# Moving the first group's values to GpSimd's queue in an attention-and-experts kernel: cast in the transfer, sink rows by a second transfer, mask fills on VectorE

## The chip, the cores and the metric

The kernel runs on one core of a Trainium2 chip. The engines are TensorE (PE), VectorE (DVE), ScalarE (ACT), GpSimd (POOL) and SyncE (SP, which only requests transfers here); 16 DMA engines move data for all of them. The metric is the device time in microseconds of one execution, smaller is better; the median of three runs is given, and a profile of one further execution.

## The reference, cut to what matters

Two parts follow each other. The first is attention over 4 batches, 8 heads, 768 positions and head width 64; the second is a mixture of 4 experts over the 3072 resulting rows.

```python
mask   = where(is_retrieval, causal, causal & (is_sink | in_window))   # 4 sinks, window 64
a      = softmax(where(mask, q @ k.T / sqrt(64), -1e9))
x      = (a @ v)                      # -> (3072, 512) rows, heads side by side
p      = probs / (probs.sum(-1) + 1e-9)
out    = sum_e p[:, e] * (relu(x @ w1[e]) @ w2[e])     # w1[e] 512x1024, w2[e] 1024x512
```

Heads 0, 2 and 6 are retrieval heads (all earlier positions); heads 1, 3, 4, 5 and 7 are streaming heads (a window of 64, and the first 4 positions, the sinks).

## The kernel before

All inputs are float32 in DRAM, and the matmuls run in float16. The attention is cut into eight groups: a batch and half of its 768 rows (384 rows) each. The first group, batch 0 and rows 0 to 383, is the front of the program: nothing can hide it, since the experts need its output. From then on the experts' matmuls are the main stream of PE, and the steps of the other groups are put between them by a planner (`plan`, `due`) at fixed places of the program. Each engine works through its own instructions strictly in the order of the program, and waits by semaphores.

**The front.** `front()` runs a list of steps written out by hand (`FRONT`): casts of q and k from float32 rows (x), transposes of them by PE (t), copies of these into place (c), scores and exponentials (s), products with the values (v and p), and what follows them (r, l, t, y, m). Names such as ck1 mean a step and its head or pair. For pairs of streaming heads the step p first multiplies by the halves of the value tiles that hold ones, to get the sums, and then by the values: p1 for heads 1 and 5, p3 for 3 and 7; v4, v0, v6 and v2 are the others. PE takes them in the order p1, v4, v0, v6, v2, p3. The masks are added to the scores as biases `bC` (causal) and `bS` (window), which live in the tile `early`; PE adds them by a matmul with the identity `ident16`.

**Tiles of the values.** `vR` holds the retrieval heads' values, and `vS` the streaming heads'. A tile of vS has 128 rows: rows 32 to 127 are 96 positions (R0 is 32), rows 0 to 3 repeat the sinks, which are the first four positions of the head, and the rest of rows 0 to 31 must only hold finite numbers. One half of the columns is the head's 64 values, the other half holds a constant for the sums. 

**Values of the first group before.** SyncE requests them as float32 into a staging area in `hA` (`request_v`, L437 and L439), after q's (asked by ScalarE) and k's float32 rows (L454). The sinks of all heads come into `v_s32` in one small transfer (L470), and GpSimd copies them to the staging rows of every tile (`put_sinks_of_v`, L430). VectorE fills the rows 0 to 31 of the staging area with zeros first (L490). GpSimd then casts head after head into vS and vR (`cast_v`, L450), with the requests of w1(0), the first layer's weights of expert 0, between the casts.

**GpSimd's queue.** Everything that is cast on the way (weights, later q, k and v) is requested by GpSimd, in one fixed order: w1(0) in two halves of two transfers (L330), w2(0) (L354), fills for group 1 (L381), w1(1), q and k of group 1 (L232), w2(1), w1(2), values of group 1 (`load_v`, L306 and L312), and so on. `landed` makes GpSimd wait until a tile has arrived. Requests of one kind of queue use eight completion semaphores in turn, so the ninth waits until the first has landed; that holds for GpSimd's requests and, together, for those of SyncE and ScalarE. Before the values GpSimd builds the masks: it fills them and cuts them with selects (L506 to L558).

**VectorE at the start** fills the warm-up tile (L416), the ones in vR and vS, the keys' tile kS (L381), the staging zeros (L490) and `x_one`; then it takes the steps of the front.

Of the kernel before, what the change touches and what calls it, by code (L numbers as in the profile page):

```python
# [11 lines left out]
FP32 = mybir.dt.float32  # L12
FP16 = mybir.dt.float16
AF = mybir.ActivationFunctionType
ALU = mybir.AluOpType
# [4 lines left out]
def kernel(  # L20
# [33 lines left out]
    nc = tc.nc  # L54
    P = 128
    B, H, S, D = q.shape
# [4 lines left out]
    HP = H // 2  # L61
# [6 lines left out]
    RETR = (1, 0, 1, 0, 0, 0, 1, 0)  # L68

    PLACE = [(h % HP, h // HP) for h in range(H)]  # L70
    RH = [h for h in range(H) if RETR[h]]
    SH = [h for h in range(H) if not RETR[h]]
    NS = int(n_sink)
    NW = int(window)
    TK = 96
    R0 = P - TK
    TQ = TK + NW
    NT = S // TK
    TC = CH // TK
# [18 lines left out]
    gp = nc.gpsimd  # L98
# [8 lines left out]
    NR, NSH = len(RH), len(SH)  # L107
# [9 lines left out]
    hA = pers.tile([P, 5 * KT * P], FP16, name="hA")  # L117
# [12 lines left out]
    vS = vSf.rearrange("p (c t s x) -> p c t s x", c=NCH, t=TC, s=NSH)  # L130

    def windows(x):

        return x[:, 0 : WT * NSH * P].rearrange("p (t s x) -> p t s x", t=WT, s=NSH)

    ident16 = pers.tile([P, P], FP16, name="ident16")

    XS = 3 * DMP * 2 * P
    early = moe.tile([P, XS], FP16, name="early", tag="xs", bufs=1)
    warm = early[:, 1024:1536]  # L140
    bC = early[:, 1536:1792]
    bS = early[:, 1792:2272].rearrange("p (t x) -> p t x", t=3)
# [27 lines left out]
    def half(u):  # L170
        return slice(u * D, (u + 1) * D)
# [5 lines left out]
    def own_v(h):  # L177
        return half(PLACE[h][1])
# [10 lines left out]
    def v_tiles(b, c, h):  # L189

        if RETR[h]:
            return vR[b % 2][:, 3 * c : 3 * c + 3, RH.index(h), :]
        if b:
            return windows(vSf)[:, :, SH.index(h), :]
        return vS[:, c, :, SH.index(h), :]
# [10 lines left out]
    def rows_of(x, b, h, c):  # L206
        return x[b, h, c * CH : (c + 1) * CH, :].rearrange("(j p) d -> p j d", p=P)

    def tiles_of(x, b, h, c):
        return x[b, h, c * CH : (c + 1) * CH, :].rearrange("(t r) d -> r t d", r=TK)  # L210

    def windows_of(x, b, h, c):

        assert b > 0
        first = ((b * H + h) * S + c * CH - WO) * D
        return bass.AP(x.tensor, x.offset + first, [[D, P], [WQ * D, WT], [1, D]])
# [85 lines left out]
    def load_v(b, c, heads):  # L302
        for h in heads:
            t = v_tiles(b, c, h)
            if RETR[h]:
                gp.dma_start(out=t[:, :, 0:D], in_=rows_of(v, b, h, c))  # L306
            elif b:
                gp.dma_start(  # L308
                    out=t[:, :, own_v(h)], in_=windows_of(v, b, h, c)
                )  # L310
            else:
                gp.dma_start(  # L312
                    out=t[R0:P, :, own_v(h)],
                    in_=tiles_of(v, b, h, c),
                )

    def sink_rows(b, c):
# [3 lines left out]
        for t in range(TC):  # L321
            nc.sync.dma_start(
                out=vS[0:NS, c, t, :, :], in_=vS[R0 : R0 + NS, 0, 0, :, :]
            )

    def load_w1(e, chunks=(0, 2)):
        x = moe_w1[e].rearrange("(u c d) f -> u d c f", u=2, c=DMP)
        for c in chunks:
            for u in range(2):
                gp.dma_start(  # L330
                    out=w1sb[half(u), e * DMP + c : e * DMP + c + 2, :],
                    in_=x[u, :, c : c + 2, :],
                )
# [33 lines left out]
    ONES = 0.0078125 * (1.0 + 15360.0 * 2.0**-23)  # L367
# [3 lines left out]
    def fill(eng, ap, value):  # L371
        ap = ap.bitcast(FP32)
        if eng is nc.scalar:
            src = ones[0 : ap.shape[0], :]
            if len(ap.shape) == 3:
                src = src.rearrange("p (a b) -> p a b", a=1)
            elif len(ap.shape) == 4:
                src = src.rearrange("p (a b c) -> p a b c", a=1, b=1)
            eng.copy(out=ap, in_=src.to_broadcast(list(ap.shape)))
        else:  # L380
            eng.memset(ap, value)  # L381
# [11 lines left out]
    def one_values_r(eng, i, c):  # L393
        t = slice(3 * c, 3 * c + 3)
        fill(eng, vR[i][:, t, :, D : D + 2], ONES)

    def one_values(eng, c):

        one_values_r(eng, 0, c)
        x = vS[:, c, :, :, :]  # L400
        if c:
            fill(eng, x[0:R0, :, :, :].rearrange("p t s x -> p (t s x)"), ONES)
        fill(eng, x[:, :, 0:2, D:P], ONES)
        fill(eng, x[:, :, 2:5, 0:D], ONES)

# [6 lines left out]
        return x.rearrange("p (s x) -> p s x", s=HP)  # L412

    q32, k32 = rows32(0), rows32(1)
    for x in (warm[:, 0:P], warm[:, P:]):
        nc.vector.memset(x.bitcast(FP32), 0.0)  # L416
    v32 = hA[:, 12 * H * D :].bitcast(FP32)
    vR32 = v32[:, 0 : NR * 3 * D].rearrange("p (n j d) -> p n j d", n=NR, j=3)
    vS32 = v32[:, NR * 3 * D : (NR * 3 + NSH * TC) * D]
    zeros = vS32[0:R0, :]  # L420
    vS32 = vS32.rearrange("p (n t d) -> p n t d", n=NSH, t=TC)

    STAGE = (1, 3, 5, 7, 4)

    v_s32 = early[0:NS, 0:1024].bitcast(FP32).rearrange("p (h d) -> p h d", h=H)

    def put_sinks_of_v():
        for n, m, x in ((0, HP, v_s32[:, 1:H:2, :]), (HP, 1, v_s32[:, HP : HP + 1, :])):
            x = x.rearrange("p n (t d) -> p n t d", t=1)
            gp.tensor_copy(  # L430
                out=vS32[0:NS, n : n + m, :, :], in_=x.to_broadcast([NS, m, TC, D])
            )

    def request_v(eng, heads):
        for h in heads:
            if RETR[h]:
                eng.dma_start(out=vR32[:, RH.index(h), :, :], in_=rows_of(v, 0, h, 0))  # L437
            else:
                eng.dma_start(  # L439
                    out=vS32[R0:P, STAGE.index(h), :, :], in_=tiles_of(v, 0, h, 0)  # L440
                )

    def cast_v(eng, heads):
        for h in heads:
            if RETR[h]:
                out_, in_ = v_tiles(0, 0, h)[:, :, 0:D], vR32[:, RH.index(h), :, :]
            else:
                out_ = v_tiles(0, 0, h)[:, :, own_v(h)]
                in_ = vS32[:, STAGE.index(h), :, :]
            eng.tensor_copy(out=out_, in_=in_)  # L450

    def request_triples(eng, x, x32, s):
        y = x[0, 2 * s : 2 * s + 2, 0:CH, :]
        eng.dma_start(  # L454
# [4 lines left out]
    for s in (0, 2, 1, 3):  # L459
# [7 lines left out]
    )  # L467
    request_triples(nc.sync, k, k32, 0)
    request_triples(nc.sync, k, k32, 2)
    nc.sync.dma_start(out=v_s32, in_=v[0, :, 0:NS, :].rearrange("h r d -> r h d"))  # L470
    request_triples(nc.sync, k, k32, 1)
    request_triples(nc.sync, k, k32, 3)
    request_v(nc.sync, (1, 5, 4, 0, 6, 2, 3, 7))
    nothing = warm.bitcast(FP32)[:, 0:1]
    x = kR[0][:, 0, :, :, :].rearrange("p n t x -> p (n t x)").bitcast(FP32)
    nc.scalar.copy(out=x, in_=nothing.to_broadcast(list(x.shape)))
    nc.sync.dma_start(
        out=probs,
        in_=moe_domain_probs[0 : NPL * P, :].rearrange("(t p) e -> p t e", p=P),
    )  # L480
    nc.sync.dma_start(
        out=p_in.rearrange("t x e -> t (x e)"),
        in_=moe_domain_probs.rearrange("(t x) e -> t (x e)", x=P),
    )
    nc.vector.memset(eps, 1e-9)
    nc.vector.memset(ones, ONES)
    make_identity(nc, ident16)
    one_values(nc.vector, 0)
    zero_keys(nc.vector, 0)
    nc.vector.memset(zeros, 0.0)  # L490


    ps_warm = pO.tile([P, DM], FP32, name="pO", bufs=2)
# [7 lines left out]

    def mask_c(x, keep, drop):

        gp.memset(x, keep)  # L506
        for i in range(2):
            gp.affine_select(
                out=x[:, i * P : (i + 1) * P], in_=x[:, i * P : (i + 1) * P],
                compare_op=ALU.is_ge, fill=drop, base=0, pattern=[[1, P]],  # L510
                channel_multiplier=-1,
            )

    def mask_s(x, n, keep, drop):

        gp.memset(x, keep)
        gp.affine_select(
            out=x, in_=x, compare_op=ALU.is_ge, fill=drop,
            base=R0, pattern=[[0, n], [1, TQ]], channel_multiplier=-1,
        )  # L520
        gp.affine_select(
            out=x, in_=x, compare_op=ALU.is_ge, fill=drop,
            base=NW - 1 - R0, pattern=[[0, n], [-1, TQ]], channel_multiplier=1,
        )
        gp.memset(x[0:R0, :, :], drop)
        gp.memset(x[0:NS, :, 0:TK], keep)
        gp.affine_select(
            out=x[0:NS, 0, 0:TK], in_=x[0:NS, 0, 0:TK], compare_op=ALU.is_ge,
            fill=drop, base=-NW, pattern=[[1, TK]], channel_multiplier=-1,
        )  # L530

    def mask_w():
# [20 lines left out]
            base=WQ - WF - NW, pattern=[[1, WQ]], channel_multiplier=-1,  # L553
        )

    mask_c(bC, 0.0, -60000.0)
    mask_s(bS[:, 0:2, :], 2, 0.0, -60000.0)
    gp.tensor_copy(out=bS[:, 2, :], in_=bS[:, 1, :])  # L558
    put_sinks_of_v()
    k16 = moe.tile([P, H, 3, D], FP16, name="k16", tag="pB", bufs=1)  # L560
    qt16 = att.tile([P, H, 3, D], FP16, name="q16", bufs=1)

# [9 lines left out]
        return w2sb[0:1, (e + 1) * FTP - 1, 0:1]  # L572


    cast_v(gp, (1,))
    load_w1(0, (0,))
    cast_v(gp, (5, 4, 0))
    load_w1(0, (2,))
    cast_v(gp, (6, 2, 3, 7))
    load_w2(0)  # L580
    zero(gp, kR[0][:, 1, :, :, :])
    zero_keys(gp, 1)
# [1254 lines left out]
```

## Time and profile before

| what | us |
|---|---|
| median of 3 runs | 373.56 (372.93 to 374.04) |
| the profiled execution | 373.37 |
| its span (first to last instruction) | 371.6 |
| PE busy | 365.0 |
| VectorE busy | 279.8 |
| ScalarE busy | 227.0 |
| GpSimd busy | 118.7 |
| granted clock of TensorE | 1.0 throughout |

The page gives busy times for the whole span, and the span in 40 slices of 9.3 us, as tenths. The trace can also be asked for one engine's instructions in order of time (the timeline), for the chain of work that ended last, and for who waited for whom. In the timeline a line gives the start, the length, the engine, the line of the program, the operation, the tiles, and in brackets the idle time just before with what ended it. Matmuls are pipelined, so a busy PE is not PE at its peak.

### The profile page before, as it was taken

What the parts mean: (1) busy time and instruction counts of PE and PEld (TensorE: products, weight loads), DVE (VectorE), ACT (ScalarE), POOL (GpSimd) and SP (SyncE); (2) the same over time, 40 slices, a digit from 0 to 9 for tenths busy, and PEclk for the clock granted to TensorE, in tenths of its full rate; (3) what the DMA queues carried; (4) which work ended last, traced back from release to release, by engine and by line L of the source; (5) the groups of instructions that cost most, each with busy time, mean ns of one, the idle gap of its engine ahead of it and who ended that gap; (6) DMA issues with size and microseconds to landing.
All of it is one profiled execution on the core that took longest, in us unless ns stands there. A gap on an engine that the chain in (4) does not pass through costs nothing.

```text
span 371.6 us, 10363 instructions
## 1 busy us (share of the span) xinstructions
PE 365.0 (98%) x4240; PEld 310.4 (84%) x4240; DVE 279.8 (75%) x586; ACT 227.0 (61%) x476; POOL 118.7 (32%) x173
## 2 busy tenths in 40 slices
PE   8999999999999999999999999999999999999996
PEld 5744566578998989999989899998899998998996
DVE  7864785898697589778657849867768868979882
ACT  6735779357777785775776856774777361451630
POOL 6975656784075049026402740220000000000000
PEclk9999999999999999999999999999999999999999
DMA  8999999999999399969906991960220300300101
GB/s 220 176 194 208 174 198 172 188 195 131 125 110 152 87 104 145 141 98 90 175 11 76 157 152 27 127 127 6 73 69 2 114 3 2 116 2 10 50 3 56
DMA packets 119716, 39.65 MB, mean 107 GB/s; under 512 B 107648, under 2 KB 112324, under 8 KB 119668
## 3 DMA queue, kind: packets, MB, share of 16 engines
q0 software_dynamic: 82816, 18.62, 58.8%
q1 hardware_dynamic: 35764, 19.58, 25.2%
q10 hardware_dynamic: 1088, 0.79, 0.7%
q8 instruction: 33, 0.54, 0.6%
q14 instruction: 15, 0.12, 0.1%
HBM read 44.89 MB, written 6.34 MB: 138 GB/s over the span
## 4 chain that ended last, share of the span: by engine, by line
PE 82%; DMA 11%; POOL 4%; DVE 1%; issue 1%; ACT 0%; SPq 0%; POOLq 0%
PE pO L1569 31%; PE pA L1386 23%; PE pO L1415 9%; DMA w1sb<-in_moe_w_dram 5%; PE pA L893 4%; PE pO L1269 3%; PE pA L1224 3%; DMA q<-in_q_dram 2%; PE pV L1415 2%; PE pA L1415 2%; DMA w2sb<-in_moe_w_dram 2%; POOL w1sb L330 2%; PE pV L1003 2%; PE pV L951 2%; DMA hA<-in_v_dram 1%; DMA hA<-in_q_dram 1%
## 5 line engine op out<-in xcount | busy, mean ns | idle before, releaser
L1569 PEld LDWEIGHTS <-hA 128*128 128x128 f16 x1104 | 104.8, 98 | 11.9
L1386 PE MATMUL pA<-xs,w1sb 128*128 128x256 f16 x768 | 97.1, 272 | 0.0
L1386 PEld LDWEIGHTS <-w1sb 128*128 128x128 f16 x768 | 71.7, 98 | 7.3
L1569 PE MATMUL pO<-w2sb,hA 128*128 128x256 f16 x640 | 76.8, 272 | 0.0
L1395 ACT ACTIVATE hA<-pA 128x512 f16<-128x512 f32 x96 | 57.2, 598 | 28.9 <-PE pA L1386 26.6
L911 ACT ACTIVATE es<-pA 128x384 f16<-128x384 f32 (+2 forms) x122 | 58.3, 513 | 25.0 <-PE pA L893 22.1
L308 POOL DMA_DIRECT2D vS<-in_v_dram x30 | 29.6, 988 | 106.6 <-PE pV L1003 106.0
L1569 PE MATMUL pO<-tsb,hA 128*128 128x256 f16 x464 | 56.8, 272 | 0.0
L1334 DVE TENSOR_TENSOR xs<-xT,pB 128x1024 f16<-128x1024 f16 (+1 forms) x49 | 47.5, 987 | 1.9 <-DMA vS<-in_v_dram 1.9
L1152 DVE TENSOR_TENSOR hA<-hA 128x1024 f16<-128x1024 f16 x60 | 39.4, 685 | 0.6 <-PE pO L1569 0.3
L1251 ACT ACTIVATE hA<-pA 128x128 f16<-128x128 f32 (+1 forms) x61 | 20.4, 381 | 20.4 <-PE pA L1224 20.1
L1415 PEld LDWEIGHTS <-w1sb 128*128 128x128 f16 x512 | 31.4, 98 | 1.4 <-issue 0.5
L1224 PE MATMUL pA<-xT,w1sb 128*128 128x128 f16 (+1 forms) x244 | 29.3, 270 | 0.5 <-DMA w1sb<-in_moe_w_dram 0.5
L1269 PE MATMUL pO<-w2sb,hA 128*128 128x512 f16 x120 | 28.6, 379 | 1.1 <-DMA w2sb<-in_moe_w_dram 1.1
L1589 ACT COPY s<-pO 128x256 f32<-128x256 f32 x31 | 11.6, 373 | 27.3 <-PE pO L1569 21.8
L1224 PEld LDWEIGHTS <-w1sb 128*128 128x128 f16 x256 | 19.3, 98 | 9.7 <-issue 1.8
L1024 DVE TENSOR_TENSOR xT<-pV,rc 64x384 f16<-64x384 f32 x35 | 19.4, 555 | 9.5 <-ACT rc L1021 8.9
L1432 DVE CUSTOM_DVE_ANT_0 hA<-pO,s 128x512 f16<-128x512 f32 x26 | 17.7, 688 | 9.8 <-PE pO L1415 8.5
L922 DVE TENSOR_TENSOR es<-es,mS 128x384 f16<-128x384 f16 (+1 forms) x40 | 13.6, 345 | 14.9 <-ACT es L911 14.8
L1425 ACT COPY s<-pO 128x512 f32<-128x512 f32 x39 | 22.7, 587 | 3.2 <-PE pO L1415 3.0
L1018 ACT ACTIVATE rc<-pV,eps 64x384 f32<-64x384 f32 x35 | 20.2, 576 | 6.3 <-PE pV L1003 5.7
L1269 PEld LDWEIGHTS <-hA 128*128 128x128 f16 x128 | 12.1, 98 | 13.6 <-issue 1.6
(189 smaller groups left out, 545.6 us busy)
## 6 DMA issues: line engine op xcount, KB each, us to landing
pB<-p_rows SPq DMA_DIRECT2D x10, 512.0 KB
out_dram<-o SPq DMA_DIRECT2D x19, 256.0 KB
w1sb<-in_moe_w_dram POOLq DMA_DIRECT2D x16, 256.0 KB, 7.2
w2sb<-in_moe_w_dram POOLq DMA_DIRECT2D x8, 512.0 KB, 9.4
vS<-in_v_dram POOLq DMA_DIRECT2D x30, 112.0 KB, 4.8
k_rows<-in_k_dram POOLq DMA_DIRECT2D x18, 128.0 KB, 5.6
q<-in_q_dram POOLq DMA_DIRECT2D x18, 128.0 KB, 6.5
out_dram<-hA SPq DMA_DIRECT2D x4, 256.0 KB
```

Source lines behind the costliest of these rows:

```text
L308: gp.dma_start(out=t[:, :, own_v(h)], in_=windows_of(v, b, h, c))
L911: nc.scalar.activation(out=es[:, 0:cols], in_=ps[:, 0:cols], func=AF.Exp, scale=SC)
L1152: nc.vector.tensor_tensor(out=out, in0=a, in1=b, op=ALU.subtract)
L1224: nc.tensor.matmul(out=ps[:, 0 : x.shape[2]], lhsT=w1_tile(e, CTS[n], ft), rhs=x[:, CTS[n], :], start=(n == 0), stop=(n == DMP - 1),)
L1251: nc.scalar.activation(out=hs[:, ft, :], in_=ps[:, 0:cols_n], func=AF.Relu)
L1269: nc.tensor.matmul(out=ps_o, lhsT=hs[:, ft, j * P : (j + 1) * P], rhs=w2sb[:, e * FTP + ft, :], start=(ft == 0), stop=(ft == FTP - 1),)
L1334: nc.vector.tensor_tensor(out=o, in0=xin, in1=pb.to_broadcast([P, DMP, n, P]), op=ALU.mult)
L1386: nc.tensor.matmul(out=ps[:, f * PC : (f + 1) * PC], lhsT=w1_tile(e, ct, f0 + f), rhs=xs[:, ct, :], start=(ct == 0), stop=(ct == DMP - 1),)
L1395: nc.scalar.activation(out=blocks[:, b0 : b0 + 2, k0 : k0 + 2, :].rearrange("p t f x -> p f t x"), in_=ps.rearrange("p (f t x) -> p f t x" ...
L1415: nc.tensor.matmul(out=ps[:, f * P : (f + 1) * P], lhsT=w_tile(e, w[:, ct, :], f), rhs=a[:, ct, :], start=(first and f == 0 and ct == 0), ...
L1425: nc.scalar.copy(out=kept[n], in_=ps)
L1569: nc.tensor.matmul(out=ps, lhsT=a[:, k, :], rhs=b(k), start=(first and k == 0), stop=(k == KT - 1), skip_group_check=not first,)
```

## The change

The values of the first group no longer pass a staging area. GpSimd requests them straight from DRAM into vS and vR, and the transfer casts them (`load_v(0, 0, ...)`). Their sinks are copied by SyncE, head by head, out of the landed rows 32 to 35 of the head's first tile into rows 0 to 3 of all four tiles (`own_sinks`), for heads 1, 5, 4, 3 and 7. VectorE fills rows 0 to 31 of vS with the constant that the ones have. The identity's and masks' fills, and two copies inside the masks, go to VectorE; GpSimd keeps the selects, and no longer builds the causal mask twice. The requests stand in this order on GpSimd: select of the identity, three selects of the masks, heads 1 and 5, the select of the first sinks, heads 4 and 0, w1(0)'s first half, heads 3, 7, 6, 2, w1(0)'s second half, w2(0). Everything behind this is in the same order as before on every engine; the lines of the new program are some 26 lower from there on (L1224 becomes L1198).

```diff
+    def own_sinks(h):
+        x = vS[:, 0, :, SH.index(h), own_v(h)]
+        src = x[R0 : R0 + NS, 0:1, :]
+        nc.sync.dma_start(out=x[0:NS, :, :], in_=src.to_broadcast([NS, TC, D]))
...
-        if c:
-            fill(eng, x[0:R0, :, :, :].rearrange("p t s x -> p (t s x)"), ONES)
+        fill(eng, x[0:R0, :, :, :].rearrange("p t s x -> p (t s x)"), ONES)
...
-    for x in (warm[:, 0:P], warm[:, P:]):
+    masks = early[:, 1536:2272]
+    for x in (warm[:, 0:P], warm[:, P:], ident16, masks):
         nc.vector.memset(x.bitcast(FP32), 0.0)
...
-    nc.sync.dma_start(out=v_s32, in_=v[0, :, 0:NS, :].rearrange("h r d -> r h d"))
     request_triples(nc.sync, k, k32, 1)
     request_triples(nc.sync, k, k32, 3)
-    request_v(nc.sync, (1, 5, 4, 0, 6, 2, 3, 7))
...
-    make_identity(nc, ident16)
+    make_identity(nc, ident16, nomemset=True)
     one_values(nc.vector, 0)
     zero_keys(nc.vector, 0)
-    nc.vector.memset(zeros, 0.0)
...
+    def mask_c():
+        x = bC[:, 0:P]
+        gp.affine_select(out=x, in_=x, compare_op=ALU.is_ge, fill=DROP, ...)
+        nc.vector.tensor_copy(out=bC[:, P : 2 * P], in_=x)
+    def mask_s():
+        x = bS[:, 0:2, :]
+        gp.affine_select(...)        # two selects, as before
+        nc.vector.memset(x[0:R0, :, :], DROP)
+        nc.vector.memset(x[0:NS, :, 0:TK], 0.0)
+        nc.vector.tensor_copy(out=bS[:, 2, :], in_=bS[:, 1, :])
+    def mask_first_sinks():
+        x = bS[0:NS, 0, 0:TK]
+        gp.affine_select(...)        # one select, as before
...
-    mask_c(bC, 0.0, -60000.0)
-    mask_s(bS[:, 0:2, :], 2, 0.0, -60000.0)
-    gp.tensor_copy(out=bS[:, 2, :], in_=bS[:, 1, :])
-    put_sinks_of_v()
+    mask_c()
+    mask_s()
+    load_v(0, 0, (1, 5))
+    mask_first_sinks()
+    load_v(0, 0, (4, 0))
...
-    cast_v(gp, (1,))
     load_w1(0, (0,))
-    cast_v(gp, (5, 4, 0))
+    load_v(0, 0, (3, 7, 6, 2))
     load_w1(0, (2,))
-    cast_v(gp, (6, 2, 3, 7))
+    for h in (1, 5, 4, 3, 7):
+        own_sinks(h)
     load_w2(0)
```

More of the change, by code (lines that the diff above doesn't have):

```diff
@@ L414 @@
     q32, k32 = rows32(0), rows32(1)
-    for x in (warm[:, 0:P], warm[:, P:]):
+    masks = early[:, 1536:2272]
+    for x in (warm[:, 0:P], warm[:, P:], ident16, masks):
         nc.vector.memset(x.bitcast(FP32), 0.0)
[L417 to L450, printed above, removed]
     def request_triples(eng, x, x32, s):
@@ L500, in warm_up @@
             )
[L504 to L516, printed above, removed]
-        gp.affine_select(
-            out=x, in_=x, compare_op=ALU.is_ge, fill=drop,
-            base=R0, pattern=[[0, n], [1, TQ]], channel_multiplier=-1,
+    DROP = -60000.0
+    def mask_c():
+        x = bC[:, 0:P]
+        gp.affine_select(
+            out=x, in_=x, compare_op=ALU.is_ge, fill=DROP, base=0,
+            pattern=[[1, P]], channel_multiplier=-1,
+        )
+        nc.vector.tensor_copy(out=bC[:, P : 2 * P], in_=x)
+    def mask_s():
+        x = bS[:, 0:2, :]
+        gp.affine_select(
+            out=x, in_=x, compare_op=ALU.is_ge, fill=DROP,
+            base=R0, pattern=[[0, 2], [1, TQ]], channel_multiplier=-1,
         )
         gp.affine_select(
-            out=x, in_=x, compare_op=ALU.is_ge, fill=drop,
-            base=NW - 1 - R0, pattern=[[0, n], [-1, TQ]], channel_multiplier=1,
-        )
-        gp.memset(x[0:R0, :, :], drop)
-        gp.memset(x[0:NS, :, 0:TK], keep)
+            out=x, in_=x, compare_op=ALU.is_ge, fill=DROP,
+            base=NW - 1 - R0, pattern=[[0, 2], [-1, TQ]], channel_multiplier=1,
+        )
+        nc.vector.memset(x[0:R0, :, :], DROP)
[3 more added lines that the diff above has]
+        x = bS[0:NS, 0, 0:TK]
         gp.affine_select(
-            out=x[0:NS, 0, 0:TK], in_=x[0:NS, 0, 0:TK], compare_op=ALU.is_ge,
-            fill=drop, base=-NW, pattern=[[1, TK]], channel_multiplier=-1,
+            out=x, in_=x, compare_op=ALU.is_ge, fill=DROP, base=-NW,
+            pattern=[[1, TK]], channel_multiplier=-1,
         )
```

## The prediction

> **What bounds the kernel now.** I read the page first: its span and the slices.
>
> ```profile
> span 371.6 us, 10363 instructions
> PE   8999999999999999999999999999999999999996
> DMA  8999999999999399969906991960220300300101
> ```
>
> TensorE (PE) is full from the first slice on, DMA for the first 15 slices of 9.3 us. A change in the first 20 us can only move the end if it moves PE. So I read PE's timeline from 10 to 62 us for every idle stretch that a transfer or an engine ended.
>
> ```profile
> 11.51 0.44 PE L734 MATMUL pO<-es,vS 128*64 128x160 f16 x7 [0.16 <-POOL vS L450]
> ...
> 24.82 1.89 PE L1269 MATMUL pO<-w2sb,hA 128*128 128x512 f16 x8 [0.47 <-DMA w2sb<-in_moe_w_dram]
> ...
> 30.11 2.76 PE L1224 MATMUL pA<-xT,w1sb 128*128 128x384 f16 x16 [0.30 <-DMA w1sb<-in_moe_w_dram]
> ...
> 37.56 1.89 PE L1269 MATMUL pO<-w2sb,hA 128*128 128x512 f16 x8 [0.61 <-DMA w2sb<-in_moe_w_dram]
> ...
> 59.69 0.49 PE L1224 MATMUL pA<-xT,w1sb 128*128 128x384 f16 x2 [0.24 <-DMA w1sb<-in_moe_w_dram]
> ```
>
> In brackets stands the idle time before an instruction and what ended it. PE starts the MoE's first matmul at 17.2 and waits for weights four times: 0.47 + 0.30 + 0.61 + 0.24 = 1.62 us. These waits are the cushion of everything below: a PE that leaves the front later meets weights that are there. After 59.7 the chain of waits is PE nearly without a break. Up to there it runs through transfers (start, length, what):
>
> ```profile
> 4.65 4.38 DMA hA<-in_v_dram
> 9.15 0.47 POOL vS L450
> ...
> 23.00 9.10 DMA q<-in_q_dram
> ...
> 34.43 8.03 DMA w1sb<-in_moe_w_dram
> 42.74 6.41 DMA w2sb<-in_moe_w_dram
> 49.44 10.12 DMA w1sb<-in_moe_w_dram
> ```
>
> So the weights' order is paced by GpSimd's (POOL's) queue, whose first pieces wait for the values. Last, VectorE (DVE) at the start:
>
> ```profile
> 3.47 1.12 DVE L490 MEMSET hA<- 32x1280 f32 x1 [0.20 <-issue]
> 4.57 0.14 DVE L1716 MEMSET x_one<- 128x96 uint32 x1
> 4.63 0.28 DVE L631 CAST t1sb<-hA 128x384 f16<-128x384 f32 x1
> 5.87 0.56 DVE L658 CAST kS<-pA 64x384 f16<-64x384 f32 x1 [0.95 <-PE pA L642]
> ```
>
> The first cast of keys starts when DVE's fills end, with no wait for the landing: the fills set the start of the front (PE begins its transposes at 4.97).
>
> **VectorE.** Removed: the zeros of the staging rows, 1.12. Added in its place: the ones in vS's first 32 rows, the same 32x1280 shape, 1.12. These cancel. Added besides: fills of 64 and 368 columns, 320 columns by 32 rows, 96 columns by 4 rows, and copies of 128 and 160 columns. A 1280-column fill takes 1.12 and a 96-column one 0.14, so about 0.06 + 0.83 ns a column, and the 0.06 is mostly hidden behind the next. Fills: 0.06 + 0.31 + 0.33 + 0.14 = 0.84. The copies: the cast of 384 columns takes 0.28, POOL's own copy of 160 columns 0.31. So 0.1 to 0.3 each; I take 0.15, since DVE does them, 0.3 for both. Two of these wait for the one before on the same engine, 0.05 each. Sum 1.2 (0.9 to 1.6). POOL's selects between them are done by 3.1, ahead of DVE's need at 5. The first cast therefore starts at 5.85, not 4.63. Behind it stand tk0, ck1, the scores and the eight exponentials that keep ScalarE (ACT) full from 7.46 to 10.24. ACT is the limit of that stretch, so DVE's later 0.36 of waiting for keys doesn't give the time back. Front +1.2.
>
> **SyncE.** Removed: nine requests of values. The fourth key request no longer waits for a q landing (the chain shows it sent at 4.24). The keys land earlier, but behind a DVE that reaches them only at 9.7 this gives nothing.
>
> **GpSimd.** Removed: nine fills, selects and copies of masks or sinks, and eight casts (five of 0.42, three of 0.36). Added: eight requests at the row of the same transfer in group 1 (L312, 0.68; L306, 0.75). Its new times: three selects from 1.4 to 3.1 (0.29 + 2 x 0.46 and gaps). The request of head 1 waits for DVE's ones in vS, to 3.75. Heads 1 and 5 go by 5.1. The select of the first sinks waits for DVE's last fill, near 5.65, and everything behind it on POOL with it: heads 4 and 0 at 6.2 to 7.6. Then w1(0)'s first half 7.6 to 8.95 (9.70 before), 3, 7, 6, 2 to 11.8, the second half to 13 (13.2 before). w2(0) must wait until w1(0)'s first piece has landed, because eight completion counters are used in turn: 7.6 + 6.3 (that request's own landing before) = 13.9, then two requests of 0.72 to 15.3 (15.9 before). The fills and w1(1) behind come 0.6 earlier. DMA is full in this time, so what is gained is the stretch before 9.7 in which w1 wasn't yet asked for: weights earlier by 0.6 to 2. That is enough to hold the cushion, and PE can't use more.
>
> **The values' way.** Before, PE waited 0.16 for POOL's cast of head 5 (0.3 with the weight load); this goes. Now heads 1, 5, 4 (then 3, 7) need a landing and then a second transfer for the sinks. A values transfer of this size took 4.7 to 8.8 from request to landing at 40 to 46 us; the shortest of the same line family (L308, 112 KB, at 245 us) took 3.3. At 4 to 8 us the engines still finish q and k, at 324 GB/s to 7 us. I take 4.2, nearer to the quiet row, since little is queued ahead. Head 1 lands at 8, 5 at 8.6, 4 at 10.3. The second hop: SyncE's copies of sinks in group 1 (L322) issue in 0.58; the last store of the kernel goes out at 369.1 and the span ends at 371.6, 2.5; the early sinks (L470, asked for at 1.83, in POOL's hands at 5.83) took 4.0. I take 2.7. Sinks of 1, 5, 4 at 10.7, 11.3, 13.0. PE wants the first two at 11.2 + 1.2 = 12.4 (no wait) and head 4 at 11.55 + 1.2 = 12.75. Expected wait 0.5, as the end is uncertain by 1 both ways and a wait can't be below 0. Heads 3 and 7 travel behind w1's first half in POOL's one queue: landing 15, sinks of 7 at 18; PE wants them near 17.9. Again about 0.5.
>
> *A page beside this.* The Trainium skill, "DMA: Bandwidth & Descriptors", section "Anatomy of one DMA", gives a POOL-issued transfer 2.0 us and its bytes. By it, as an estimate, head 4 would have its sinks at about 11.5, both waits fall out, and the sum below would be -0.6 (373.0, inside the forecast's own range). The rows from 40 to 46 us, 4.7 and more, speak for the longer way.
>
> **Sum.** Front: +1.2 - 0.2 + 0.5 + 0.5 = +2.0. Less the cushion 1.62: +0.4 at 59.7 us, and PE carries it to the end. The profiled execution took 373.37 (1.77 around the span), so 373.8; the median of the runs, 373.56, is 0.19 above it: 374.0.
>
> **Rivals.** *The second hop becomes the wait (slower).* At the upper ends, head 4 lands at 11.9 (5.6, as one such load at 40 us) and the hop takes 3.0: sinks at 14.9, PE 2.2 late there; heads 3 and 7 add 0.5. Front +3.7, end +2.1: 375.7. It decides from a front delay of 2.7 (2.7 - 1.62 = 1.1). For it: PE takes its instructions in order, so nothing passes the waiting matmuls, and DMA is full. Against it: the quiet 3.3.
>
> *The fills are cheap and the weights come earlier (faster).* If DVE overlaps its small fills (0.6 in all) and no value is late, the front costs +0.4 and the cushion's 1.62 is nearly all gained: -1.2, 372.4. For it: three tiny fills started within 0.03 us (1.16 to 1.19). Against: the long ones are paid by the column. More than 1.62 isn't to be had here, so it is bounded.
>
> *POOL's requests are held up by DVE.* w1(0)'s first request took 0.76 beside DVE's four casts of 8.74 to 10.11, the usual one 0.60. Were requests held for those whole casts, 1.37, then head 7's sinks and heads 6 and 2 would be late by that much: front +3.4, end +1.8, 375.4. The 0.16 seen speaks against most of it.
> The Trainium skill has this as a rule ("SBUF — State Buffer", "SBUF: two separate sides"): a DVE copy in its two-port mode locks GpSimd out of writing a transfer's descriptors, while requests of SyncE or ScalarE are free of it, which speaks against moving the values. The 0.76 agrees with a short lock only.
>
> **How the numbers follow.** 0.3% (1.1 us) is about what a measurement of this kernel can tell from no change. Forecast 0.42 (its own range 373.0 to 374.7); second hop 0.33; held requests 0.07; cheap fills 0.18. Faster 0.18, same 0.42, slower 0.40. Range: from near the bounded gain, 372.5, to the second hop with head 7 a little later, 376.2.
>
> **What would show it.** DVE's first key cast near 5.85; PE's transposes from 6.2; a PE wait at the values of head 4 (L661) or of 3 and 7 (L708) put down to a vS transfer; first MoE matmul (L1198) at 19.2, not 17.2; the four weight waits gone. It is wrong if that matmul starts before 17.7 (faster), past 19.9 (slower), or if the weight waits stay although the front is late: then the supply moved too.

## The result, and the profile after

The changed kernel takes 375.91 us (median of 6 runs, 375.26 to 377.42) against 373.47 (6 runs, 372.44 to 374.04) for the kernel before on the same chip: a ratio of 1.0072, interval 1.0048 to 1.0096. It is slower by 2.4 us. The forecast of 374.0 ("no change", chance 0.42) was not what came; the time lies inside the range, at the price that the rival of the second hop had given (375.7, chance 0.33), though not by that rival's sizes.

The profiled execution took 377.42, the longest of the six. From its page, the span and the slices:

```profile
span 375.7 us, 10352 instructions
PE   6799999999999999999999999999999999999996
PEclk9889999999999999999999999999999999999999
DMA  9999999999799569989904991951220300300101
```

PE is no longer full in the first two slices (6 and 7, before 8 and 9), and the clock row, 9 or more throughout before, has an 8 in the second and third slice. All else is as it was, so the loss is in the first 25 us. PE's timeline there:

```profile
6.44 1.50 PE L616 MATMUL pA<-ident,t1sb 128*64 128x128 f16 x24 [1.67 <-DVE t1sb L605]
...
14.35 0.23 PE L708 MATMUL pO<-es,vS 128*64 128x160 f16 x1 [2.01 <-DMA vR<-in_v_dram]
14.87 0.41 PE L708 MATMUL pO<-es,vS 128*64 128x160 f16 x7 [0.30 <-DMA vR<-in_v_dram]
15.21 1.51 PE L661 MATMUL pV<-vS,es 128*96 128x66 f16 x7
...
23.18 1.46 PE L1198 MATMUL pA<-xT,w1sb 128*128 128x384 f16 x8
```

The step p1 multiplies by the ones first, ending at 12.34, and then PE stands for 2.01 us before the values of head 1 and for 0.30 before those of head 5. The view names a transfer of vR as releaser; by the program the matmul waits for the landing of head 1 and for the copy of its sinks, and only the second comes so late. The MoE's first matmul is at 23.18, against 17.22. None of the four weight waits is left: the longest pieces of the chain of waits behind 23.3 are all PE's.

The requests and VectorE's start, from the timeline of all engines:

```profile
1.92 1.92 DVE L386 MEMSET vS<- 32x1280 f32 x3 [0.20 <-issue]
4.15 1.49 POOL L312 DMA_DIRECT2D vS<-in_v_dram  x2 [1.16 <-DVE vS L386]
5.80 0.20 DVE L495 COPY early<-early 128x160 f16<-128x160 f16 x1
6.03 0.35 DVE L605 CAST t1sb<-hA 128x384 f16<-128x384 f32 x1
7.81 1.21 POOL L335 DMA_DIRECT2D w1sb<-in_moe_w_dram  x2
9.37 6.23 SPq L329 DMA_DIRECT2D vS<-vS  x5
```

GpSimd waits 1.16 for VectorE's fill of vS, then requests head 1 at 4.15. Its values land at 9.37, which is when SyncE sends the copy of the sinks. PE uses them at 14.35. The second hop took 5.0 us.

The same profile by stretches of 2 us (columns: stretch, then busy us of PE, PEld, DVE, ACT and POOL, the granted clock, the DMA share, which can exceed 1, and GB/s):

```profile
10.00:12.00 2.00, 2.00 (x37) 1.82 (x35) 1.64 (x6) 1.82 (x6) 2.00 (x4) 1.00 1.00 165
12.00:14.00 2.00, 0.34 (x10) 0.18 (x6) 1.57 (x4) 1.44 (x3) 1.82 (x3) 1.00 1.75 161
14.00:16.00 2.00, 1.36 (x12) 0.93 (x12) 0.00 (x0) 0.00 (x0) 1.72 (x4) 0.82 1.22 143
16.00:18.00 2.00, 2.00 (x17) 1.56 (x17) 0.75 (x3) 0.60 (x2) 1.99 (x6) 0.50 1.05 183
...
20.00:22.00 2.00, 2.00 (x24) 1.58 (x21) 1.16 (x4) 1.11 (x4) 1.96 (x5) 0.50 1.11 206
22.00:24.00 2.00, 1.93 (x28) 1.35 (x26) 1.32 (x5) 1.33 (x3) 0.71 (x1) 0.98 1.10 203
```

In this execution the granted clock falls to 0.50 behind the wait and stays there to about 22, so a second loss follows the first. It isn't needed for the result: the three executions whose recorded clock is 1.00 on average took 375.26, 375.40 and 375.84, still 1.8 us and more above the kernel before; two at 0.995 took 375.98 and 376.36, and the profiled one, at 0.991, took 377.42.

### The profile page after: what moved, and what is told of

The parts are those of the page before. It is cut to its first block, busy times and chain, and to the rows that moved or that the text cites. A ratio compares the mean times of both kernels' runs of the same rounds, so it can differ in the third digit from the quotient of the medians.

```text
span 375.7 us, 10352 instructions
## 1 busy us (share of the span) xinstructions
PE 366.8 (98%) x4240; PEld 312.1 (83%) x4240; DVE 279.4 (74%) x592; ACT 227.7 (61%) x476; POOL 117.2 (31%) x164
## 3 DMA queue, kind: packets, MB, share of 16 engines
q1 hardware_dynamic: 32628, 18.79, 22.4%
## 4 chain that ended last, share of the span: by engine, by line
PE 92%; DMA 4%; DVE 2%; POOL 1%; issue 0%; ACT 0%; POOLq 0%
PE pO L1543 31%; PE pA L1360 22%; PE pO L1389 9%; PE pO L1243 7%; PE pA L1198 7%; PE pA L867 5%; DMA w2sb<-in_moe_w_dram 2%; PE pV L1389 2%; PE pA L1389 2%; PE pV L925 2%; PE pV L977 2%; DMA w1sb<-in_moe_w_dram 1%; DVE xs L1308 1%; PE pA L1635 0%; DVE vS L386 0%; PE pA L1243 0%
## 5 line engine op out<-in xcount | busy, mean ns | idle before, releaser
L1543 PEld LDWEIGHTS <-hA 128*128 128x128 f16 x1104 | 104.8, 98 | 11.9
L1198 PE MATMUL pA<-xT,w1sb 128*128 128x128 f16 (+1 forms) x244 | 28.9, 270 | 0.0
L1198 PEld LDWEIGHTS <-w1sb 128*128 128x128 f16 x256 | 19.5, 98 | 8.5 <-issue 0.2
L867 PE MATMUL pA<-qT,kR 128*128 128x128 f16 (+2 forms) x141 | 23.7, 267 | 0.0
```

The lines of the kernel that those rows point to most:

```text
L867: nc.tensor.matmul(out=ps[:, o : o + nq], lhsT=key_tile(b, c, h, t), rhs=qTs[b, c][:, hp, q0 : q0 + nq], start=(n == 0 or not first), stop ...
L1198: nc.tensor.matmul(out=ps[:, 0 : x.shape[2]], lhsT=w1_tile(e, CTS[n], ft), rhs=x[:, CTS[n], :], start=(n == 0), stop=(n == DMP - 1),)
L1543: nc.tensor.matmul(out=ps, lhsT=a[:, k, :], rhs=b(k), start=(first and k == 0), stop=(k == KT - 1), skip_group_check=not first,)
```

## The experiments

Twelve kernels were run, each timed beside the kernel before on its chip (372.8 to 373.0 there, 373.47 beside the changed kernel). So kernels from different chips are compared by their ratios to it, not by their medians. One relation serves for reading them all. Where no weight wait is left, the span ends 352.3 to 352.6 us after the MoE's first matmul in nine profiles of this study (18.24 gives 370.6, 21.65 gives 374.2, 23.18 gives 375.7); only the quiet hop below, whose weights start late, stands apart. In the kernel before, 17.22 gives 371.6, so 354.4. The cushion is therefore worth 2.0, not the 1.62 that the prediction summed.

**The sinks' copies left out.**
```diff
-    for h in (1, 5, 4, 3, 7):
-        own_sinks(h)
```


> The kernel after without the five copies of sinks (rows 0 to 3 of the first group's streaming tiles then hold the constant of the fills, so that part of the attention is left out). Theory of the second hop: PE's wait ahead of the values of heads 1, 5 and 4 (2.0 + 0.3 us in the profile of after, then a slowed clock) goes, the clock stays at 1.0, the first MoE matmul starts at 18.2 to 18.7 (23.2 in after, 17.2 before), and with the weight waits of 1.6 us swallowed the time is 373.0 to 373.6. Rival, the values themselves land too late on GpSimd's queue: PE still waits 1 us or more at the same place and the time stays at 375 or above. Rival, the fills on VectorE are the cost: 374.8 to 375.5.

372.53 (11 runs), ratio 0.9994 [0.9983, 1.0006]. No wait at p1, first MoE matmul 18.79, no weight waits. The clock did not stay at 1.0 as expected: behind a gap of 2.02 us ahead of the first transposes it read 0.50 from 8 to 10. The landings alone are early enough; everything that made the kernel slower hangs on the copies. The time is a little below what was expected, since the cushion is larger.

**The fills alone**, on the kernel before: masks' and identity's fills and two copies by VectorE, values as before.
```diff
-    for x in (warm[:, 0:P], warm[:, P:]):
+    for x in (warm[:, 0:P], warm[:, P:], ident16, masks):
...
-    make_identity(nc, ident16)
+    make_identity(nc, ident16, nomemset=True)
```


> The kernel before with one part of the change alone: the fills and two copies of the masks and the identity on VectorE, the selects on GpSimd; the values still come through the staging area. Theory (fills delay the front, the weight waits swallow it): first cast of keys at 5.8 to 6.1 instead of 4.63, first MoE matmul at 18.2 to 18.6, weight waits down from 1.6 to about 0.4 us, time 373.3 to 373.8. Rival, no cushion: 374.6 to 374.9. Rival, the fills cost nothing: first MoE matmul at 17.2 to 17.5.

372.93, 0.9996 [0.9986, 1.0006]. The first cast was at 5.92 and the first MoE matmul at 19.24, later than expected, for a reason in PE's timeline:

```profile
6.33 2.77 PE L649 MATMUL pA<-ident,t1sb 128*64 128x128 f16 x24 [1.56 <-DVE t1sb L638]
...
9.76 0.41 PE L912 MATMUL pA<-early,ident 128*128 128x256 f16 x1
...
11.07 0.27 PE L912 MATMUL pA<-early,ident 128*128 128x256 f16 x1
```

The same 24 transposes took 1.50 in the changed kernel's profile. They ran at half the clock here: a mask matmul of 256 columns took 0.41 before about 10.4 and 0.27 after it, the two lengths that the changed kernel's profile shows inside and outside its stretch at 0.50. The clock row prints 1.00 all the same, because the trace's record of the clock begins only at 10.41 in this run (at 5.03 in the changed kernel's, at 6.19 in the one before). All weight waits were gone, so the whole cushion paid for it and the time stood still.

**The front late by itself**, on the kernel before, with PE kept busy by more warm-up matmuls.
```diff
-    nc.vector.memset(zeros, 0.0)
+    for _ in range(3):
+        nc.vector.memset(zeros, 0.0)
...
-    warm_up(ps_warm, 7, 512)
+    warm_up(ps_warm, 19, 512)
```


> The kernel before with VectorE's zeros of the staging rows written three times instead of once, and twelve more warm-up matmuls of 512 columns so that PE isn't idle in the time gained. It only delays the front, by 2 x 1.32 = 2.6 us. Theory of the cushion: the first MoE matmul starts at 19.8, all four weight waits (1.62 us) go, and the time is 1.0 above before: 374.2 to 374.8. Rival, no cushion: +2.6, 376.1. Rival, the weights set everything up to 60 us: +0, 373.5.

373.67, 1.0022 [1.0013, 1.0030]. First MoE matmul 19.75 (2.5 late), all weight waits gone, time +0.7 (+1.0 was expected): 1.8 to 2.0 of delay are free. Transposes took 1.50 here, without idle time in front of them.

**The hop replaced**, all else as in the changed kernel: SyncE fetches the sink rows of all heads from DRAM at the very start, and GpSimd copies them into vS.
```diff
-    for h in (1, 5, 4, 3, 7):
-        own_sinks(h)
+    nc.sync.dma_start(out=v_s32, in_=v[0, :, 0:NS, :].rearrange("h r d -> r h d"))
...
+    put_sinks_of_v()          # three copies, 4x512 each
     load_v(0, 0, (1, 5))
```


> The kernel after with only the second hop taken away: all sinks in one small float32 transfer asked for first by SyncE, copied into vS by GpSimd (three copies, 1.5 us) ahead of head 1's request; VectorE's fills stay as in after. Theory (the end follows the first MoE matmul, 352.4 us from it to the end of the span once no weight wait is left): first cast at 6.0, no wait at heads 1, 5, 4, first MoE matmul at 18.7 to 19.3, span 371.1 to 371.7, time 372.8 to 373.5. Rival, GpSimd's copies cost as much as the hop did, since the requests behind them are 0.8 us later: a wait of 1 us or more at a head's values and 374.3 or more.

373.10 (10 runs), 1.0007 [0.9996, 1.0017]. Its profiled execution was the longest of its runs (374.01): 2.77 for the transposes again, 1.04 of waiting for head 2, and the first MoE matmul at 20.01 (18.7 to 19.3 was expected). Still, by the ratios (1.0072 against 1.0007) the hop alone is 0.65%, 2.4 us, and what is left of the loss, 0.07%, isn't clear of noise.

**The hop replaced, and GpSimd fills rows 0 to 31 of vS** in its idle first microsecond.
```diff
-        fill(eng, x[0:R0, :, :, :].rearrange("p t s x -> p (t s x)"), ONES)
+        fill(gp, x[0:R0, :, :, :].rearrange("p t s x -> p (t s x)"), ONES)
```


> The kernel after with the two suspected costs taken away: the sinks of all heads come in one small float32 transfer, asked for first by SyncE, and GpSimd copies them straight into vS (three copies) ahead of its first request, so that no transfer waits for another; and the fill of vS's rows 0 to 31 goes to GpSimd, ahead of its selects. Theory (hop and fills are the cost, GpSimd's earlier requests a gain): first cast at 4.7 to 4.9, no wait at heads 1, 5 and 4, perhaps 0.5 us at head 6 (queued behind w1 and heads 3, 7), first MoE matmul at 17.2 to 17.9, weight waits nearly gone, time 372.2 to 372.9, better than before. Rival, the weights' arrival is set by bandwidth alone: waits of 1 us and more stay, 373.3 to 373.8.

372.42 (12 runs), 0.9989 [0.9979, 0.9999], the only kernel whose interval lies below 1. First cast 5.04, no wait at heads 1, 5 and 4. One is left, at head 6 (1.21, where 0.5 was expected), whose request now stands behind the copies:

```profile
15.60 0.36 PE L671 MATMUL pV<-vR,es 128*128 128x65 f16 x6 [1.21 <-DMA vR<-in_v_dram]
18.24 0.98 PE L1208 MATMUL pA<-xT,w1sb 128*128 128x384 f16 x5
```

**Heads 6 and 2 ahead of 3 and 7**, on top of that.
```diff
-    load_v(0, 0, (3, 7, 6, 2))
+    load_v(0, 0, (6, 2, 3, 7))
```


> The version without hop and with the fill on GpSimd (372.4), with the order of four requests changed: heads 6 and 2 ahead of 3 and 7, as PE wants them. Theory: the 1.21 us that PE waited for head 6 go, the first MoE matmul starts at 17.0 to 17.4 instead of 18.24, and as GpSimd's requests of weights are earlier than in before, few weight waits come back (under 0.6 us): time 371.2 to 371.9, faster than both kernels. Rival, the weights take over as the limit: waits of 1 us or more on w1sb or w2sb and 372.3 to 372.6, no gain over the order before.

372.41, 0.9985 [0.9969, 1.0002]; expected was a gain of 0.5 or more. The wait at head 6 is gone, but in the profile ScalarE waited 1.57 for the keys (cast at 7.18), and PE began the MoE at 17.98.

**w1(0)'s first half behind the values**, in the changed kernel.
```diff
-    load_w1(0, (0,))
     load_v(0, 0, (3, 7, 6, 2))
+    load_w1(0, (0,))
     load_w1(0, (2,))
```


> The kernel after with w1(0)'s first half asked for behind the values of heads 3, 7, 6 and 2 instead of ahead of them; the second hop stays. It asks why the copies of head 1's sinks took 5.0 us from request (9.37) to PE (14.35), where 2.7 was forecast. Theory, the hop is slowed by the weights' traffic: with w1 asked for at 10.4 at the earliest, the hop takes 2.3 to 3.5 us, PE goes on at 12.0 to 12.9, and the time falls to 372.8 to 373.8. Rival, five microseconds are what such a transfer of small rows takes beside any traffic of this queue: PE goes on at 14 or later and the time stays at 375.2 to 376.

375.91, 1.0078 [1.0051, 1.0104]: the time is that of the changed kernel, not the expected 372.8 to 373.8. The transposes took 2.77, so PE came to p1 late and no wait shows there, but 1.21 at head 4. The time alone would clear w1, but the traffic does not. A view of a stretch counts its packets by size and by queue; q1 is SyncE's queue, which carries nothing but these copies here. First the changed kernel, from the request of head 1's copy (9.37) to 12.7, where no line for q1 stands, and from 12.7 to 14.5; then this run, from that request (9.84) to 11.4, again without q1, and from 11.4 to 11.9:

```profile
DMA packets 413, 0.49 MB, mean 149 GB/s; under 512 B 181, under 2 KB 181, under 8 KB 413
...
q1 hardware_dynamic: 60, 0.01, 3.3%
...
DMA packets 875, 0.11 MB, mean 69 GB/s; under 512 B 875, under 2 KB 875, under 8 KB 875
...
q1 hardware_dynamic: 20, 0.00, 6.3%
```

In the changed kernel no packet of the three copies moves for 3.4 us, while the weights' packets of 2 KB do. Here only the values' small packets travel, at a DMA share of 1.12 up to 11.5, and all 20 packets of head 1's copy have moved 2.1 us after the request. Head 4's copy, sent at 11.50 behind w1's requests (10.67), is used 4.9 later, at 16.35. So w1's transfers do slow the hop, and taking them out of head 1's way only moved the wait to head 4. Whether the size of the weights' packets does it or something else about them was not separated.

**PE kept busy in the wait**, in the changed kernel: ten matmuls of 512 columns of zeros between p1's sums and its values.
```diff
             for ps, other in zip(tiles, (1, 0)):
+                if other == 0 and heads == (1, 5):
+                    warm_up(pV.tile([P, 512], FP32, name="pV", bufs=2), 10, 512)
```


> The kernel after with ten matmuls of 512 columns on zeros (2.1 us) put between the sums and the values of heads 1 and 5, where PE otherwise waits 2.0 us and more for the sinks. Nothing is sped up by them but the clock. Theory: part of the loss of after is TensorE's granted clock, which fell to 0.5 from 14.5 to 22 us behind this wait in the profile: here it stays at 1.0 there, the first MoE matmul starts at 20.5 to 21.2 (23.2 in the profile of after), and the time is 374.9 to 375.4 with little spread between executions (375.3 to 377.4 in after). Rival, the clock plays no part in the median: 375.7 to 376.1.

375.71 (375.46 to 375.90), 1.0073 [1.0057, 1.0088]; granted clock 1.0 from 12 on, first MoE matmul 21.47. The spread is 0.4 us, against 2.2 in the changed kernel. The median did not move. It isn't a clean price of the clock: the transposes took 2.77 here, and the added matmuls ended at 15.8, about 1 us after the changed kernel had its sinks and 2 us after the last packets of its own three copies (60 of q1 from 12.5 to 13.7).

**Values first.** As the best so far, with the values of heads 1, 5, 4 and 0 requested ahead of GpSimd's three copies, and the sink rows behind k's first two requests.
```diff
-    put_sinks_of_v()
     load_v(0, 0, (1, 5))
     mask_first_sinks()
     load_v(0, 0, (4, 0))
+    put_sinks_of_v()
     load_w1(0, (0,))
     load_v(0, 0, (6, 2, 3, 7))
```


> No second hop (sink rows by one small transfer from DRAM and three copies by GpSimd), GpSimd fills rows 0 to 31 of vS, heads 6 and 2 ahead of 3 and 7, and now the values of heads 1, 5, 4 and 0 are requested ahead of GpSimd's three copies (1.5 us), and the sink rows behind k's first two requests. Theory (the front is what the late or early values and VectorE's start make it): no wait for values, first cast near 5.0, first MoE matmul near 17.3, a weight wait of up to 0.5 back, span 370.0 to 370.4, time 371.8 to 372.3. Rival (the front's own chain holds it at 17.9 or later whatever the values do): as the version with heads 6 and 2 first, 372.4.

372.57 (12 runs), 0.9995 [0.9983, 1.0007]; first MoE matmul 18.08. The rival's side. Head 6, requested at 9.41, made PE wait 1.15 at 15.45, a way of 6.0 us.

**Smaller copies**, in the changed kernel.
```diff
-        nc.sync.dma_start(out=x[0:NS, :, :], in_=src.to_broadcast([NS, TC, D]))
+        nc.sync.dma_start(out=x[0:NS, 0:1, :], in_=src)
```


> The changed kernel, but each second transfer copies the sinks into one of the four tiles instead of four (the sinks of the other three tiles are left out of the attention): a quarter of the bytes and of the pieces. If the size of the second transfer sets its way (theory B), PE uses head 1's sinks some 2 us earlier, at about 12.3, first MoE matmul near 20.5, time 373.5 to 374.3. If it is the fixed way of a small transfer in a busy system (theory A), it stays near 4.5 to 5.0 us from request to use, first MoE matmul 21.3 to 23.2, time 375.2 to 376.0.

374.46, 1.0045 [1.0026, 1.0064], between the two theories: by the ratios 1.0 us below the changed kernel, with intervals that overlap. Its PE came to p1 late (transposes 2.77) and waited 0.30 for head 5:

```profile
9.45 5.63 SPq L329 DMA_DIRECT2D vS<-vS  x5
...
14.11 0.41 PE L708 MATMUL pO<-es,vS 128*64 128x160 f16 x7 [0.30 <-DMA vS<-vS]
19.88 1.46 PE L1198 MATMUL pA<-xT,w1sb 128*128 128x384 f16 x8
```

Head 5's values go 0.76 earlier than in the changed kernel (14.87). No packet of q1 moves before 12.7 here either; the 24 of the three copies have then moved by 14.0, the changed kernel's 60 by 14.5. So size counts a little, and only once the copies are under way. From head 5's values to the MoE this profile needs 5.77, the changed kernel's 8.31: 2.5 us is what the halved clock took in that one execution.

**The hop in a quiet system.** In the changed kernel GpSimd requests nothing behind heads 1, 5, 4 and 0 until their sinks have arrived.
```diff
+    for h in (1, 5, 4):
+        own_sinks(h)
+    for h in (1, 5, 4):
+        landed(vS[0:1, 0, TC - 1, SH.index(h), own_v(h)][:, 0:1])
     load_w1(0, (0,))
     load_v(0, 0, (3, 7, 6, 2))
```


> The changed kernel, but GpSimd requests nothing behind heads 1, 5, 4 and 0 (no weights, no other values) until the sinks of heads 1, 5 and 4 have arrived, so that the second transfers run with hardly any traffic beside them. If other transfers' traffic makes the 5.0 us (theory B), the way falls to 2.5 to 3 us and head 1's values are used near 12.3; if not (theory A) it stays at 4.5 or more and head 1's values are used at 14 or later. The end is late in both (w1(0) is asked for 5 to 8 us later than in the changed kernel): first MoE matmul 23 to 27, time 376 to 380.

383.76, 1.0283 [1.0257, 1.0308]: as a kernel worse, since weights and the other values start 5 us later. As a measurement it settles that the hop is short without traffic. Its timeline and its stretches:

```profile
9.29 11.08 SPq L329 DMA_DIRECT2D vS<-vS  x5
11.22 0.18 POOL L539 COPY seen<-vS 1x1 f16<-1x1 f16 x1 [3.40 <-DMA vS<-vS]
...
24.85 0.31 PE L712 MATMUL pO<-es,vS 128*64 128x160 f16 x1 [2.12 <-DMA vS<-vS]
```
```profile
10.00:12.00 2.00, 2.00 (x37) 1.82 (x35) 1.47 (x6) 1.82 (x6) 0.18 (x1) 1.00 0.01 2
12.00:14.00 2.00, 1.86 (x28) 1.39 (x25) 1.64 (x5) 1.44 (x3) 1.08 (x4) 1.00 0.04 9
```

Head 1's sinks are requested at 9.29 and seen at 11.22: 1.9 us with a DMA share of 0.01, where the changed kernel needed 5.0 with 1.00 and 1.75. PE does not wait for heads 1, 5 and 4. The same run shows the long way too: head 3's copy, sent at 18.99 beside the weights that were asked for by then, moves no packet before 23, and PE waits 2.12 for it, up to 24.85, 5.9 after the request. The weights' traffic makes the hop long; with the values alone beside it, as in the run with w1 behind, head 1's copy was nearly as short as here.

The Trainium skill, "DMA: Bandwidth & Descriptors", section "Anatomy of one DMA — SWDGE (gpsimd) path", gives a transfer a fixed 2.0 us plus its bytes. It states this for GpSimd's transfers; the quiet 1.9 of SyncE's agrees with it, the 5.0 beside traffic does not.

**The copies of the sinks behind heads 6 and 2**, on the version with the values first.
```diff
     load_v(0, 0, (4, 0))
-    put_sinks_of_v()
     load_w1(0, (0,))
-    load_v(0, 0, (6, 2, 3, 7))
+    load_v(0, 0, (6, 2))
+    put_sinks_of_v()
+    load_v(0, 0, (3, 7))
```


> As the version with the values requested ahead of GpSimd's copies of the sinks, but these copies (1.5 us) stand behind the requests of heads 6 and 2, so that w1(0)'s first half and heads 6 and 2 are requested 1.5 us earlier (near 6.8 and 8.0). Theory (the wait at head 6, 1.15 us, was its request at 9.4 plus 6.0 of way): the wait goes, first MoE matmul near 17.0 to 17.3, span 370.0, time 371.8 to 372.2. Rival (the way grows when the requests stand closer together, since other transfers' traffic sets it): head 6 still makes PE wait by 0.5 or more, first MoE matmul 17.7 or later, time 372.4 to 372.7.

372.94 (12 runs), 1.0004 [0.9994, 1.0014]. The wait for head 6 went, and the first MoE matmul came at 17.47, the earliest of the variants; yet the span is 371.1, longer than with 18.24:

```profile
17.47 1.46 PE L1209 MATMUL pA<-xT,w1sb 128*128 128x384 f16 x8
...
30.50 2.76 PE L1209 MATMUL pA<-xT,w1sb 128*128 128x384 f16 x16 [1.08 <-DMA w1sb<-in_moe_w_dram]
```

A weight wait of 1.08 stands where the kernel before had 0.30. No variant's profiled execution ended before 370.6: in these profiles, below a first MoE matmul of about 18, what the front gains goes back to the weights. The two versions at 372.4 remain the fastest, 0.1% below the kernel before, a difference hardly clear of noise.

## Why the prediction was right or wrong, point by point

- **VectorE, +1.2.** Right in kind: the first cast came at 6.03 instead of 5.85, +1.40, inside the bounds. The fills themselves cost the time as forecast. What was missed is that the late cast leaves PE idle in front of the first transposes (1.6 to 2.0 instead of 0.2), and that these can then run at half the clock. Of eight profiles with such a gap, five show 2.77 for the 24 transposes, one 1.93 and two 1.50; the kernel before, with its short gap, shows 2.07, which fits a clock at half up to 6.19, where its record begins.
- **GpSimd's queue.** Nearly exact: the first request of values 4.15 (3.75 forecast), w1(0) at 7.81 to 9.0 (7.6 to 8.95), the values to 11.9 (11.8), w2(0) at 13.09 and, behind a 0.46 wait for w1(0)'s landing, 14.28 (13.9 to 15.3). Weights were earlier, as forecast.
- **The landings, 4.2.** Head 1 took 5.2 from its request, head 4 3.3. So head 1, not head 4, decided. By itself this would have cost nothing: with a hop of 2.7 head 1's sinks are there at 12.07, and PE asks for them at 12.34.
- **The second hop, 2.7.** This is the step that failed. It was sized by the last store of the kernel (2.5, on idle queues) and by the early sinks (4.0), and the value nearer to the quiet row was taken, in a stretch where DMA was full. It measured 5.0, and 1.9 without traffic. A nearer row lay in the trace before: the same kind of copy for group 1 (L322), sent from 23.90 on beside the weights, of which only the issue was read; from 23.9 to 27 no packet of SyncE's queue moves there. PE waited 2.01 + 0.30 at heads 1 and 5, where "no wait" stood; at heads 4 and 3/7, where 0.5 each stood, none showed. At 3 and 7 that was luck: their copies moved only between 18.3 and 20.7, after the 17.9 at which PE was to want them, and PE was late itself, at 22.07.
- **The cushion, 1.62.** Mis-sized: 2.0 by the span relation, 1.8 to 2.0 by the late front. Where the rest of it sits isn't shown.
- **The sum.** Front +2.0 forecast; the profiled execution shows +5.96, of which 1.05 is PE's late arrival at p1, 2.31 the two waits and about 2.5 the halved clock. Without the hop the medians are 372.4 to 373.1, no change. The hop's 2.4 then passes to the end, with nothing left to absorb it.
- **The rival of the second hop** was what happened, at its price (375.7, measured 375.91), but by other sizes: not at head 4 with a hop of 3.0, but at head 1 with 5.0. So the agreement of the price is luck, and it is this rival's upper bound that kept the time inside the range. "It decides from a front delay of 2.7", which is the cushion plus the 1.1 that can be told from no change, should read 3.1, with a cushion of 2.0.
- **Held requests.** Not seen: VectorE's four casts ran from 9.47 to 10.80, beside the requests of heads 3 and 7, which took 1.38 together, 0.7 each as usual (0.67 for head 4).
- **Cheap fills and earlier weights (faster).** The weights did come earlier and the cushion was bounded as said, but the fills were paid in full. With the fill moved to GpSimd and no hop it is worth 0.1%, not 1.2 us.
- **The signs.** Late first cast, a PE wait at p1's or p3's line, weight waits gone, a first MoE matmul past 19.9 meaning slower: all there, except that the wait at that line (L708) was for heads 1 and 5, not for head 4 or 3 and 7, and that the releaser was not a vS transfer in this view. By its own last sign, 23.18 against 19.9, the forecast of no change was wrong.

Left open: what the clock adds to the median. Its 2.5 us are shown for one execution; the other five of the changed kernel took 375.26 to 376.36 (three of them at a recorded clock of 1.00) and have no timeline. That a slow start of the transposes replaced the later drop in them is only argued; as that start lies ahead of the clock's record, the recorded mean can't show it.

## What to carry to other kernels

A dependent second transfer costs its quiet 2 us only where no weights' transfers are under way; where they are, size it by the landing of such a copy in such a stretch, even for 2 KB, and not by how long its request takes. A full DMA row alone doesn't tell, since beside the values' small packets the way stayed short. Before trading an engine's copies for such a hop, see whether an idle engine can do the copies from rows fetched early. And a cushion works in both directions: it hides a late front up to its size, and hands back to the weights what an earlier front would gain.

## What the runs showed of the hardware

- After 2.01 us in which PE had no matmul, the granted clock went to 0.50 for some 6.8 us (about 15.3 to 22.1). In that stretch a 256-column matmul took 0.42 us, at full clock 0.27. The Trainium skill, "TensorE: Matmul & The Clock Gate", section "Part 1: The HAM clock gate (the "warmup" mystery)", puts the fall after an idle window of about 3.4 us. Here shorter gaps were followed by it, 2.01 us in the changed kernel and 2.02 in the one without the copies, while none followed the gap of 1.21 with w1 behind. The recorded stretches at one clock are 3.41, 6.83, 10.24 and 13.65 us long, multiples of 3.41; that the place of a gap within such steps decides is only argued.
- The granted clock's row does not show all of it. In the version with the fills alone the row reads 1.00 from 6 to 12, while transposes and mask matmuls took 1.5 to 1.8 times as long up to 10.4. The trace's record of the clock begins there, at 10.41; the row has no record before it. The length of one matmul form (0.41 or 0.27 for 256 columns) is the surer sign.
- Small copies issued by SyncE do not get through beside weights' transfers for some time: no packet moved for 3.4 us in the changed kernel, for 4.0 and more (18.99 to 23) in the quiet run's second half, against 1.4 to 1.6 us with nothing or only small packets under way (from 9.29 to 10.7, and from 9.84 to 11.4 with w1 behind).
- GpSimd's copies and VectorE's float32 casts side by side slow each other: four casts of keys took 2.06 beside three GpSimd copies of 1.91 in all (the copies of the sinks behind heads 6 and 2), against 1.33 for the casts in the changed kernel and 1.51 for the copies where they stand earlier.
